# Fused RWKV-5 attention and SoLU feed-forward block on one core: early zeros, one product, the scalings and the last store move to other engines, and two small factors move behind a join

## Chip, cores and metric

One Trainium2 chip (trn2), one core. The metric is device time in microseconds (us), the median of several executions. Three runs of the kernel before gave 323.55, 321.37 and 322.94 us, so its median is 322.94 us.

## What is computed

The reference has two stages. The first is RWKV-5 attention over 4 batches, 8 heads, 768 positions and a head width of 48:

```python
for t in range(S):
    cur = einsum('bhd,bhe->bhde', u * k[t], v[t])
    y[t] = einsum('bhd,bhde->bhe', r[t], state + cur)
    state = w * state + einsum('bhd,bhe->bhde', k[t], v[t])
```

The second takes x, the 3072 rows of 384 that the heads of y form:

```python
h = x @ w_in                       # 384 -> 1024
solu = h * softmax(h)
ln = (solu - mean) / sqrt(var + 1e-6) * g_ln
out = ln @ w_out                   # 1024 -> 384
```

All of it is in 32-bit floats; w_in, w_out and g_ln come as 64-bit floats and are converted on the chip.

## The kernel before, in words

The rows are cut into N = 24 units of 128 positions (4 batches by 6 chunks of time). All of the work is in `direct_path`; the order of the instructions on each engine is the order in which the program text calls the helpers, written out by hand for all stages (no scheduler reorders it). An engine runs its queue in order, and waits at an instruction whose operands are not ready, so that everything behind it on that engine waits too.

A unit goes through these helpers. `load` (L471) issues the transfers of k, r and v on SP's queue. `decay_k` (L718) multiplies k by a table of decays, `kdec`, on GpSimd (POOL) and gives `kp` (L721); `decay_r` (L725) does the same for r. `weigh` (L732) forms the product r·k·u in two GpSimd multiplications, L734 (k by u) and L735 (times r), into `rku`; `sum_own` (L737) sums it over the head on VectorE (DVE, L739), and `diagonal` (L744) writes those sums onto the diagonal of the score tile, for the first four units by eight ScalarE (ACT) activations (L749). `turn_r` and `turn_k` (L774, L781) transpose r and kp on TensorE (PE); `whole_scores` (L794) or `scores` (L806) multiply them; `take_scores` (L822) copies the upper part of the scores over the diagonal tile on DVE (L827, L832). `whole_y` or `merged_y` multiply with v (L858, L881); `outer` builds the new state (L913) and `middle` and `update` add it (L934, L947, L949). `take_y` (L887) brings y to `xT` on ACT (L892); `ffn_in` (L962) multiplies it with w_in into the one `h_ps` tile (L969); `exponential` (L974) takes the exponential on ACT (L977), `unit_a` (L1046) forms solu on DVE (L1053), and only then can the next unit's `ffn_in` overwrite `h_ps`. `unit_b` (L1057) takes the squares on ACT (L1064, L1065). `halve_ln` (L1124) splits the words in halves (L1127), a transposing transfer turns them (L1116), and `join_ln` (L1130, L1121) puts the words together on DVE. `row_sums_12` (L1197) forms two sums of turned rows (L1201, L1202), which TensorE needs for the products in `both_a` to `both_d` (L1211) with w_out. `variance`, `root` and `shifts` (L1071, L1075, L1079) give the factors that `normalise` (L1098, ACT, L1102) applies.

Before the units stands the setup: an identity, tables of decays built by doubling on DVE (L648 to L654), `turn_table` (L662), which transposes a table on PE and copies it on ACT to `kdec` (L665), and the zeros: six tiles `vts` hold v, and their second halves (`vt[:, 1]`, 128 by 512 words) are zeroed by one ACT activation each (L641). ACT reaches the copy to `kdec` only behind the six. `spin` (L615) issues matmuls on PE whose result is not used.

The weights come in 14 pieces. `convert_a` to `convert_d` (L531 to L572) take the low words on ACT (L537), the high words on DVE (L550, L552), add on POOL (L560), and, for the eight pieces of w_out, scale by -g (`minus_g`): pieces of odd number on ACT (L568), of even number on DVE (L571). The scalings stand in the loop at L1399, in its four later passes, two pieces each.

At the end, `both_c` (L1265) and `both_d` (L1279) add up and store the last two units. For the last pair, `both_d` copies the left 192 columns on DVE (L1284) and stores them by SP (L1285). Every engine then reads a flag (L1842) and branches over a fallback path (L1843) that isn't taken; SP waits for all transfers and engines (L1870).

Of the kernel before, what the change touches and what calls it, by code (L numbers as in the profile page):

```python
# [9 lines left out]
F32 = mybir.dt.float32  # L10
# [389 lines left out]
def direct_path(  # L400
# [29 lines left out]
    nc = tc.nc  # L430
    B, H, S, D = r.shape
# [18 lines left out]
    apool = ctx.enter_context(tc.tile_pool(name="apool", bufs=2))  # L450
# [15 lines left out]
    NLD, NV = 5, 6  # L466
    rpads = [const.tile([128, H, P], F32, name=f"rpad{i}") for i in range(NLD)]
    kpads = [const.tile([128, H, P], F32, name=f"kpad{i}") for i in range(NLD)]
    vts = [const.tile([128, 2, H, P], F32, name=f"vt{i}") for i in range(NV)]
# [70 lines left out]
    def convert_b(j):  # L540
        hi, low = step[j]
        n = low.shape[1]
        ma = wpool.tile([128, n], U32, tag="ma", name="ma", bufs=4)
        part = ma
        if pieces[j][2] is None:
            part = psM.tile([128, n], F32, tag="m", name="part").bitcast(U32)

        nc.vector.tensor_scalar(out=part, in0=hi, scalar1=3, scalar2=0x3FFFFFF8,  # L550
                                op0=ALU.logical_shift_left, op1=ALU.bitwise_and)
        nc.vector.scalar_tensor_tensor(out=ma, in0=hi, scalar=0xC0000000, in1=part,  # L552
                                       op0=ALU.bitwise_and, op1=ALU.bitwise_or)
        step[j] = ma, low
# [8 lines left out]
    def convert_d(j, scalar=False):  # L563
        dst, _, f = pieces[j]
        ma, low = step.pop(j)
        if f is not None:
            if scalar:
                nc.scalar.activation(out=dst, in_=ma.bitcast(F32), func=ACT.Copy,  # L568
                                     scale=minus_g[:, f : f + 1])
            else:  # L570
                nc.vector.tensor_scalar_mul(out=dst, in0=ma.bitcast(F32),  # L571
                                            scalar1=minus_g[:, f : f + 1])  # L572
# [64 lines left out]
    u_ps = psM.tile([128, dm], F32, tag="m", name="u_ps")  # L637
    nc.tensor.matmul(u_ps, ones_row, u_row, start=True, stop=True)
    nc.scalar.copy(out=u_bc.rearrange("p h d -> p (h d)"), in_=u_ps)
    for vt in vts:  # L640
        nc.scalar.activation(out=vt[:, 1].rearrange("p h x -> p (h x)"),  # L641
                             in_=ident[:, 0:1].to_broadcast([128, H * P]), func=ACT.Copy, scale=0.0)
    nc.vector.tensor_scalar(out=pw[:, 0, 0], in0=wd_ps, scalar1=LOW, scalar2=HIGH,
# [2 lines left out]
    for j in range(8):  # L646
# [5 lines left out]
        else:  # L652
            n = 1 << (j - 1)
# [54 lines left out]

    ones = const.tile([128, 1], F32, name="ones")
    nc.gpsimd.memset(ones, 1.0)  # L710

    live = {}

# [4 lines left out]
    def decay_k(i):  # L718
        X = live.setdefault(i, {})
        X["kp"] = apool.tile([128, H, P], F32, name="kp", bufs=5)  # L720
        nc.gpsimd.tensor_mul(X["kp"].rearrange("p h d -> p (h d)"),  # L721
                             kpads[i % NLD].rearrange("p h d -> p (h d)"),
                             kdec.rearrange("p a d -> p (a d)"))
# [5 lines left out]
                             rpads[i % NLD].rearrange("p h d -> p (h d)"),  # L729
                             rdec.rearrange("p a d -> p (a d)"))  # L730

    def weigh(i, engine):  # L732
        rku = live[i]["rku"] = apool.tile([128, H, D], F32, name="rku")
        engine.tensor_mul(rku, kpads[i % NLD][:, :, 0:D], u_bc)  # L734
        engine.tensor_mul(rku, rku, rpads[i % NLD][:, :, 0:D])  # L735

    def sum_own(i):  # L737
        own = live[i]["own"] = small.tile([128, H, 1], F32, name="own")
# [223 lines left out]
    def ffn_in(i, halves=(0, 1), units=True):  # L962
        X = live[i]
        if 0 in halves:
            X["h"] = psH.tile([128, dff], F32, tag="h", name="h_ps")
        h_ps = X["h"]
        for n in halves:
            for j in range(KD):
                nc.tensor.matmul(h_ps[:, ts(n, NX)], X["xT"][:, j, :], w_in_sb[:, j, ts(n, NX)],  # L969
                                 start=(j == 0), stop=(j == KD - 1))  # L970
        if 1 in halves and units:
            exponential(i)
# [94 lines left out]
    def unit(i):  # L1067
        unit_a(i)
        unit_b(i)
# [9 lines left out]
    def shifts(i, j, engine):  # L1079
        i = max(i, SEVEN)  # L1080
        if i < j:
            tot, shift, scale, rstd = (stats[:, n, i:j] for n in (1, 2, 3, 4))
            engine.tensor_scalar(out=scale, in0=rstd, scalar1=-float(dff), scalar2=1.0,
                                 op0=ALU.mult, op1=ALU.mult)
            engine.tensor_tensor(out=shift, in0=tot, in1=rstd, op=ALU.mult)  # L1085
# [34 lines left out]
    def join(words, turned):  # L1120
        nc.vector.tensor_copy(out=words.bitcast(U16).rearrange("p n (t o) -> p o n t", o=2),  # L1121
                              in_=turned)
# [7 lines left out]
    def join_ln(i):  # L1130
        X = live[i]
        if i not in ROOM:
            X["lnT"] = fpool.tile([128, KF, 128], F32, name="lnT")
        else:
            X["lnT"] = bigs[ROOM[i]].rearrange("p (f t) -> p f t", f=KF)
        join(X["lnT"], X["turned"])
# [36 lines left out]
    KH, NH = KF // 2, dm // 2  # L1173
    left, right = slice(0, NH), slice(NH, dm)
# [34 lines left out]
    def block(dst, rows, weights, start=False):  # L1209
        for f in range(KH):  # L1210
            nc.tensor.matmul(dst, rows[:, f], weights[:, f], start=(start and f == 0),  # L1211
                             stop=(f == KH - 1), skip_group_check=True)
# [52 lines left out]
    def both_c(i):  # L1265
        X, Y = live.pop(i), live.pop(i + 1)
        ending[i] = X
        o, o2, a, e = (X[n] for n in ("o", "o2", "a", "e"))
        rows, rows2 = (out[ds(b * S + c * T, T)] for b, c in (units[i], units[i + 1]))
        if not X.get("summed"):  # L1270
            nc.vector.tensor_tensor(out=o2[:, right], in0=a, in1=o2[:, right], op=ALU.add)
        block(a, Y["lnT"][:, KH:KF], sums_w[4])
        if i + 2 == N:
            nc.sync.dma_start(out=rows2[:, right], in_=o2[:, right])
        if X.get("summed") != 2:
            nc.vector.tensor_tensor(out=o[:, right], in0=e, in1=o[:, right], op=ALU.add)
        nc.sync.dma_start(out=rows, in_=o)

    def both_d(i):  # L1279
        X = ending.pop(i)  # L1280
        (b, c), o2, a = units[i + 1], X["o2"], X["a"]
        rows2 = out[ds(b * S + c * T, T)]
        if i + 2 == N:
            nc.vector.tensor_copy(out=o2[:, left], in_=a)  # L1284
            nc.sync.dma_start(out=rows2[:, left], in_=o2[:, left])  # L1285
        else:
            nc.scalar.copy(out=o2[:, left], in_=a)
            nc.sync.dma_start(out=rows2, in_=o2)
# [31 lines left out]
    for q in range(2):  # L1320
        rows = slice(q * P, q * P + D)
        nc.gpsimd.tensor_tensor(out=wide.rearrange("p (a q) -> p a q", q=2)[P : P + D, :, q],
                                in0=back[rows, :, 0], in1=pw[rows, 0, 0], op=ALU.mult)
    weigh(0, nc.gpsimd)
    decay_k(0)
    sum_own(0)
    diagonal(0)
# [1 line left out]
    spin(2)  # L1329
    whole_scores(0)  # L1330
    convert_b(0)
    decay_k(1)
    weigh(1, nc.gpsimd)
    turn_r(1)
    spin(4)
# [63 lines left out]
    for i in range(LA, LA + LO):  # L1399
        j = i - LA  # L1400
        load(i + 5, "kr")
        load(i + 4, "v")
        if i > LA:
            ffn_in(j)
        before, now = now, [todo.pop(0) for _ in range(2 if todo else 0)]
        turn_r(i + 2)
        turn_k(i + 2)
        for p in before:
            convert_c(p)
        for p in now:  # L1410
            take_up(p)
        if i > LA:
            diagonal(i + 1)
            unit(j)
        for p in before:
            convert_d(p, p % 2)
        sum_own(i + 2)
        decay_k(i + 3)
        if i + 3 >= FIRST:
            decay_r(i + 3)  # L1420
        weigh(i + 3, nc.gpsimd)
        if i - LO >= 0:
            halve_ln(i - LO)
        if i - LO - 1 >= 0:
            join_ln(i - LO - 1)
        if i + 1 < WHOLE:
            whole_scores(i + 1)
            take_scores(i + 1)
        else:
            place(i + 1)  # L1430
            attend([i + 1])
            middle(i + 1)
        if LA < i < WHOLE:
            whole_y(i)
            take_y(i)
            whole_outer(i)
        elif i >= WHOLE:
            merged_y(i)
            take_y(i)
        if i > LA:  # L1440
            update(i)
        else:
            nc.vector.tensor_single_scalar(out=minus_g, in_=g_sb, scalar=-1.0, op=ALU.mult)
        if i + 1 >= WHOLE:
            take_scores(i + 1)
        for p in now:
            convert_b(p)
        halve_rk(i + 3)
# [17 lines left out]
    i = LA + LO  # L1466
    j, l = i - LA, 0
# [41 lines left out]
    for i in range(LA + LO + 2, ELEVEN, 2):  # L1509
        j, l = i - LA, i - LA - LO  # L1510
# [8 lines left out]
        first, second = ([n] if n < N else [] for n in (i + 2, i + 3))  # L1519
# [121 lines left out]
    for i in range(ELEVEN, N - 1, 2):  # L1641
        j, l = i - LA, i - LA - LO
        one, two = turned[i]
        first, second = ([n] if n < N else [] for n in (i + 2, i + 3))
# [80 lines left out]
    i = N - 1  # L1725
    j, l = i - LA, i - LA - LO
# [68 lines left out]
    variance(i, N, nc.vector)  # L1795
    root(i, N)
    both_c(l)
    shifts(i, N, nc.vector)
    join_ln(l + 3)
    row_sums_12(l + 2)  # L1800
    row_sums_34(l + 2, nc.vector)
    both_d(l)
# [72 lines left out]
```

## Time and profile before

The profile is of one execution of 322.73 us; its trace spans 321.0 us.

| What | us or share |
|---|---|
| median of three runs | 322.94 |
| the profiled execution, its own time | 322.73 |
| span of its trace | 321.0 |
| PE busy | 307.4 (96%) |
| DVE busy | 265.9 (83%) |
| POOL busy | 245.6 (77%) |
| ACT busy | 244.4 (76%) |
| transfers, mean share of the 16 engines, 22.3 to 56 us | 0.99 |
| granted TensorE clock | 0.996 |

How to read it. "Busy" is the time in which an engine has an instruction of that kind running. The slices of the page cut the span in 40; a table of stretches gives the same per stretch that one chooses. The chain of waits walks back from the last instruction to what released it. The timeline lists instructions with their start, duration, and the idle time before them with what ended it. Matmuls are counted twice in these rows (each 32-bit matmul leaves two records), and their ends are modelled.

### The profile page before, as it was taken

How to read it: one execution, taken by the hardware profiler on the slowest of the kernel's cores; microseconds unless marked ns; L12 is line 12 of the kernel's file. 1: busy time of each engine (PE TensorE's matmuls, PEld its weight loads, DVE VectorE, ACT ScalarE, POOL GpSimd, SP SyncE). 2: the span in 40 equal slices, each digit the busy share in tenths (PEclk: the TensorE clock that was granted, in tenths of full speed). 3: DMA queues.
4: the chain of work that ended last, by engine and by line, in shares of the span. 5: the costliest groups of instructions: out<-in, count | busy, mean ns of one | idle time of the engine just before them, and what ended most of it. 6: DMA issues, size and time to landing. Idle time of an engine off the chain costs nothing.

```text
span 321.0 us, 9696 instructions
## 1 busy us (share of the span) xinstructions
PE 307.4 (96%) x3903; PEld 216.9 (68%) x3903; DVE 265.9 (83%) x449; ACT 244.4 (76%) x418; POOL 245.6 (77%) x264
## 2 busy tenths in 40 slices
PE   6989999999999999999999999999999999999992
PEld 4866566555456466687677677678768677769891
DVE  7796999998887988989889799799979946777760
ACT  3875888888559888968968969959959968788420
POOL 3999778889999999999999999979988274272000
PEclk9999999999999999999999999999999999999998
DMA  7999998778999999988999999995876445675912
GB/s 161 241 266 208 200 188 205 119 142 134 190 170 178 173 175 150 162 145 169 165 196 180 168 191 209 197 196 114 143 174 144 85 121 118 135 191 116 204 76 61
DMA packets 165780, 52.64 MB, mean 164 GB/s; under 512 B 158301, under 2 KB 161502, under 8 KB 165726
## 3 DMA queue, kind: packets, MB, share of 16 engines
q1 hardware_dynamic: 165712, 51.92, 83.3%
q8 instruction: 33, 0.54, 0.7%
q14 instruction: 21, 0.17, 0.2%
q10 hardware_dynamic: 14, 0.00, 0.0%
HBM read 26.75 MB, written 4.72 MB: 98 GB/s over the span
## 4 chain that ended last, share of the span: by engine, by line
PE 61%; POOL 18%; DVE 10%; issue 4%; DMA 3%; SPq 1%; ACT 0%; POOLq 0%; ACTq 0%
PE o_ps L1211 26%; PE h_ps L969 16%; PE h_part L1003 9%; POOL kp L721 4%; POOL rku L734 4%; POOL big L754 3%; POOL rp L728 3%; PE y_ps L881 2%; POOL rku L735 2%; PE at L819 2%; DMA vt<-in_v_dram 1%; DVE ma L552 1%; PE h_part L881 1%; DMA wq<-in_w_dram 1%; DVE big L832 1%
## 5 line engine op out<-in xcount | busy, mean ns | idle before, releaser
L969 PE MATMUL h_ps<-w_in_sb,xT 128*128 128x512 f32 x216 | 96.9, 598 | 0.0
L969 PEld LDWEIGHTS h_ps<-w_in_sb,xT 128*128 128x128 f32 x216 | 39.9, 190 | 44.9 <-issue 43.2
L1127 ACT COPY halves<-solu 128x2048 uint16<-128x2048 uint16 x23 | 43.6, 1895 | 1.9 <-DMA halves<-halves 1.7
L721 POOL TENSOR_TENSOR kp<-kpad,kdec 128x512 f32<-128x512 f32 x24 | 34.1, 1423 | 0.9 <-ACT kdec L665 0.2
L1121 DVE COPY big<-halves 128x2048 uint16<-128x2048 uint16 x21 | 33.8, 1613 | 0.6 <-DMA halves<-halves 0.3
L1121 DVE COPY lnT<-halves 128x2048 uint16<-128x2048 uint16 x18 | 31.2, 1759 | 0.0
L735 POOL TENSOR_TENSOR rku<-rku,rpad 128x384 f32<-128x384 f32 x24 | 29.2, 1218 | 1.9
L832 DVE COPY_PREDICATED big<-later_half,at 64x512 f32<-64x512 uint32 x40 | 29.5, 736 | 0.7
L734 POOL TENSOR_TENSOR rku<-kpad,u_bc 128x384 f32<-128x384 f32 x24 | 29.8, 1241 | 0.2
L754 POOL TENSOR_SCALAR_AFFINE_SELECT big<-own 64x512 f32<-64x512 f32 x40 | 27.6, 691 | 1.8
L1211 PE MATMUL o_ps<-w_out_sb,ma 128*128 128x192 f32 x160 | 28.1, 328 | 0.0
L1211 PEld LDWEIGHTS o_ps<-w_out_sb,ma 128*128 128x128 f32 x160 | 26.2, 190 | 1.9 <-issue 1.6
L728 POOL TENSOR_TENSOR rp<-rpad,rdec 128x512 f32<-128x512 f32 x15 | 25.1, 1674 | 0.0
L977 ACT ACTIVATE e<-h_ps 128x1024 f32<-128x1024 f32 x18 | 18.4, 1022 | 8.7 <-PE h_ps L969 8.6
L1061 ACT ACTIVATE e<-solu,stats 128x1024 f32<-128x1024 f32 x20 | 23.0, 1148 | 2.2 <-DVE solu L1053 2.1
L1053 DVE SCALAR_TENSOR_TENSOR solu<-h_ps,stats,e 128x1024 f32<-128x1024 f32 x18 | 23.1, 1284 | 1.5
L1102 ACT ACTIVATE solu<-solu,stats 128x1024 f32<-128x1024 f32 x17 | 21.0, 1233 | 1.0 <-POOL stats L1085 0.9
L1166 PE MATMUL o_ps<-w_out_sb,lnT 128*128 128x384 f32 x64 | 21.6, 491 | 0.0
L1072 POOL TENSOR_SCALAR stats<-stats 128x2 f32<-128x2 f32 (+2 forms) x13 | 5.9, 451 | 19.2 <-ACT e L1061 18.7
L956 POOL TENSOR_TENSOR vt<-vt,wide 48x384 f32<-48x384 f32 x16 | 19.4, 1226 | 0.8
L1211 PE MATMUL o_ps<-w_out_sb,lnT 128*128 128x192 f32 x112 | 19.8, 330 | 0.0
L1211 PEld LDWEIGHTS o_ps<-w_out_sb,lnT 128*128 128x128 f32 x112 | 18.2, 190 | 1.7 <-issue 1.4
(198 smaller groups left out, 699.2 us busy)
## 6 DMA issues: line engine op xcount, KB each, us to landing
raw<-in_moe_w_out_dram SPq DMA_DIRECT2D x16, 384.0 KB, 4.1
kpad<-in_k_dram SPq DMA_DIRECT2D x24, 192.0 KB, 5.1
rpad<-in_r_dram SPq DMA_DIRECT2D x24, 192.0 KB, 5.0
vt<-in_v_dram SPq DMA_DIRECT2D x40, 96.0 KB, 3.6
raw<-in_moe_w_in_dram SPq DMA_DIRECT2D x7, 512.0 KB, 6.7
out_dram<-o SPq DMA_DIRECT2D x18, 192.0 KB, 3.0
raw<-in_moe_w_in_dram SPq DMA_DIRECT2D x10, 256.0 KB, 3.8
out_dram<-kp SPq DMA_DIRECT2D x5, 192.0 KB, 2.5
```

The lines of the kernel that those rows point to most:

```text
L721: nc.gpsimd.tensor_mul(X["kp"].rearrange("p h d -> p (h d)"), kpads[i % NLD].rearrange("p h d -> p (h d)"), kdec.rearrange("p a d -> p (a ...
L728: nc.gpsimd.tensor_mul(X["rp"].rearrange("p h d -> p (h d)"), rpads[i % NLD].rearrange("p h d -> p (h d)"), rdec.rearrange("p a d -> p (a ...
L734: engine.tensor_mul(rku, kpads[i % NLD][:, :, 0:D], u_bc)
L735: engine.tensor_mul(rku, rku, rpads[i % NLD][:, :, 0:D])
L754: nc.gpsimd.affine_select(out=G[rows, c].rearrange("p a q u -> p (a q) u"), in_=X["own"][rows].to_broadcast([U, H, U]), compare_op=ALU.is_ ...
L832: nc.vector.copy_predicated(X["G"][rows, c].rearrange("p a q u -> p q a u"), later_half[rows].unsqueeze(1).to_broadcast([U, 2, HP, U]), X[ ...
L969: nc.tensor.matmul(h_ps[:, ts(n, NX)], X["xT"][:, j, :], w_in_sb[:, j, ts(n, NX)], start=(j == 0), stop=(j == KD - 1))
L1003: nc.tensor.matmul(dst, rows, weights, start=start, stop=True, skip_group_check=True)
L1053: nc.vector.scalar_tensor_tensor(out=solu, in0=X["h"], scalar=rs, in1=X["e"], op0=ALU.mult, op1=ALU.mult, accum_out=tot)
L1121: nc.vector.tensor_copy(out=words.bitcast(U16).rearrange("p n (t o) -> p o n t", o=2), in_=turned)
L1127: copy(out=both.rearrange("p (o n) -> p o n", o=2), in_=split(X["solu"]))
L1211: nc.tensor.matmul(dst, rows[:, f], weights[:, f], start=(start and f == 0), stop=(f == KH - 1), skip_group_check=True)
```

## The change

Six edits. (1) Only the first four v tiles get their zeros on ACT; the two others get them from two GpSimd memsets, placed behind the last of its setup memsets. (2) `weigh` takes a second engine; for unit 0 the multiplication by r is done by DVE. (3) `decay_k(1)` moves from behind `convert_b(0)` to directly behind `weigh(0)`, ahead of `decay_k(0)`. (4) All scalings of the w_out pieces go to ACT. (5) Behind `both_c` of units 18 and 19, `join_ln(l + 3)`, the join of unit 21, comes before `shifts(i, N, nc.vector)`, the factors of the last unit (L1798, L1799). (6) The last store of 192 columns is cut in two halves of 96: the first is copied by DVE and stored by SP, the second is copied by ACT and stored by ACT's queue.

```diff
-    for vt in vts:
+    for vt in vts[:4]:
         nc.scalar.activation(out=vt[:, 1].rearrange("p h x -> p (h x)"),
...
     nc.gpsimd.memset(ones, 1.0)
+    for vt in vts[4:]:
+        nc.gpsimd.memset(vt[:, 1], 0.0)
...
-    def weigh(i, engine):
-        rku = live[i]["rku"] = apool.tile([128, H, D], F32, name="rku")
+    def weigh(i, engine, second=None):
+        rku = live.setdefault(i, {})["rku"] = apool.tile([128, H, D], F32, name="rku")
         engine.tensor_mul(rku, kpads[i % NLD][:, :, 0:D], u_bc)
-        engine.tensor_mul(rku, rku, rpads[i % NLD][:, :, 0:D])
+        (second or engine).tensor_mul(rku, rku, rpads[i % NLD][:, :, 0:D])
...
         if i + 2 == N:
-            nc.vector.tensor_copy(out=o2[:, left], in_=a)
-            nc.sync.dma_start(out=rows2[:, left], in_=o2[:, left])
+            for n, (copy, store) in enumerate(((nc.vector.tensor_copy, nc.sync),
+                                               (nc.scalar.copy, nc.scalar))):
+                part = slice(n * NH // 2, (n + 1) * NH // 2)
+                copy(out=o2[:, part], in_=a[:, part])
+                store.dma_start(out=rows2[:, part], in_=o2[:, part])
...
-    weigh(0, nc.gpsimd)
+    weigh(0, nc.gpsimd, nc.vector)
+    decay_k(1)
     decay_k(0)
     sum_own(0)
...
     convert_b(0)
-    decay_k(1)
     weigh(1, nc.gpsimd)
...
         for p in before:
-            convert_d(p, p % 2)
+            convert_d(p, True)
         sum_own(i + 2)
...
     both_c(l)
+    join_ln(l + 3)
     shifts(i, N, nc.vector)
-    join_ln(l + 3)
     row_sums_12(l + 2)
```

## The prediction

> **What bounds the kernel now.** The busy shares of the page come first: PE is busy for 96% of the span, so only the stretches where PE stands still can give time back. The table of stretches shows where they are (columns: length, then PE, PEld, DVE, ACT, POOL busy with instruction counts, clock, transfer share, GB/s):
>
> ```profile
> 0.00:22.30 22.30, 17.85 (x255) 14.73 (x255) 17.46 (x58) 14.11 (x33) 16.41 (x34) 1.00 0.94 229
> 22.30:56.00 33.70, 33.70 (x475) 20.46 (x472) 29.91 (x57) 27.04 (x59) 27.79 (x29) 1.00 0.99 197
> 56.00:75.00 19.00, 17.39 (x323) 10.31 (x325) 18.35 (x32) 16.77 (x28) 16.29 (x17) 1.00 0.71 127
> ...
> 291.00:299.00 8.00, 7.44 (x46) 7.17 (x45) 7.01 (x15) 6.90 (x8) 0.68 (x2) 1.00 0.44 101
> ```
>
> PE lacks 4.45 us up to 22.3, nothing up to 56, 1.6 us from 56 to 75, 0.56 us from 291 to 299, and the last 6 us; the rows left out here (75 to 291) lack 0.8 in all. Second, PE's waits over the span (us in total, times, longest), which name who ends those gaps:
>
> ```profile
> PE kv_ps L913 <- DVE big L779: 1.3, 2, 0.7
> PE y_ps L858 <- issue: 0.7, 1, 0.7
> PE o_ps L1211 <- DVE ma L1202: 0.6, 1, 0.6
> ```
>
> The two on L779 lie at 58.1 and 67.3, with one of 0.3 on L832 at 74.6; the one on L1202 lies at 298.5.
>
> Third, the chain of waits for the start (start, us, what), and ACT's timeline beside it:
>
> ```profile
> 8.46 1.01 POOL rku L734
> 9.54 1.00 POOL rku L735
> 10.54 0.17 issue
> 10.74 2.52 POOL kp L721 x2
> ```
>
> ```profile
> 6.97 3.22 ACT L641 ACTIVATE vt<-ident 128x512 f32<-128x512 f32 x6
> 10.09 0.57 ACT L665 COPY kdec<-kd_ps 128x512 f32<-128x512 f32 x1
> ```
>
> From 8.5 to 15.3 us the chain is GpSimd's; kp needs kdec, which ACT copies only behind six zeroings. The chain is also GpSimd's from 67 to 121 us, where the change adds and removes nothing of GpSimd's; PE then runs from 128.4 to 291.
>
> **What the Trainium skill says.** "ScalarE: Activation LUTs" (What ACT_TABLE_LOAD costs) prices an activation at 186 ns + 0.833 ns per element, 93 ns more for a pointer scale: 599 ns for 384 columns; the trace's L568 takes 600. "SBUF — State Buffer" (SBUF: two separate sides) calls the pair of ports that DVE and GpSimd share an exclusive lock, held for a whole instruction, also by a DVE instruction with two SBUF inputs against GpSimd reads; that bears on the product moved to DVE. The trace agrees in kind: L728 takes 1.29 us at 77.2 and 2.33 us beside DVE's copy L1121 at 70 us. "DMA: Bandwidth & Descriptors" (Issuing engines are not separate DMA queues) says that a second queue saves only the issue time; no transfer of the trace before shows two queues near the end.
>
> **The change part by part.**
>
> Zeros, the product and the order at the start. Two zeroings less on ACT are 2 x 0.54 = 1.07 us (3.22/6): ACT is free at 9.1 instead of 10.1. kdec can then start once its transposes end: PE's kd_ps runs 8.25 to 9.31, so kdec runs about 9.36 to 9.93. GpSimd's two memsets: small ones show 98 ns for one column and 194 for 128, so 512 columns are about 0.48 us each, 1.0 in all; GpSimd idles 4.0 us before 7.94, waiting for the tables, and hides them. On DVE the product has no row of this shape; L1201, the same kind with 512 columns, takes 0.69, and smaller rows drop about 1 ns a column, so 0.55 us. Bounds: 0.5, or 1.5 if it waits for a GpSimd instruction of 1 us. DVE idles 1.39 us before L739, so it runs 9.55 to 10.1, and sum_own starts at 10.1 instead of 10.57; ACT's eight activations start 0.45 us earlier. Nothing else stands behind the product's wait on DVE before the product itself is ready (L790 ends at 9.19). kp starts at about 10.1 (the lock until the product ends) instead of 10.74: 0.6 us, though 1.0 us left GpSimd, because kdec gates. The later rows on GpSimd and DVE shift by 0.6. The new order of decay_k puts unit 1's kp 1.3 us earlier still, ready at 11.4, where PE asks for it at 13.1; kp(0) is then ready at 12.6, and its reader on PE comes at 15.5. No transfer gates: the weight piece that lands last, issued at 13.45, needs 9.1 us and is there at 22.55, DVE takes it at 24.32. PE itself idles in this stretch, behind something that moves, 0.16 (tk_ps at 13.31), 0.34 and 0.16 us (y_ps at 19.46 and 20.04): 0.66. Its 0.73 before 21.63 ended by nothing the profile names, and I leave it there. So PE can gain 0 to 0.9; I take 0.5, carried to 56, since PE has no gap there.
>
> Scalings. Four DVE instructions of 0.55 (L571, 2.2 us) become four on ACT of 0.60 less the 0.09 overlap of neighbours (2.0 to 2.4 us). ACT in passes 3 to 6, by its timeline: the exponential L977 waited 1.0 and 0.7 us for PE after the first two, which hides 0.6 us each. In the third it did not wait:
>
> ```profile
> 61.71 0.60 ACT L568 ACTIVATE w_out_sb<-ma,minus_g 128x384 f32<-128x384 f32 x1
> 62.22 1.88 ACT L1127 COPY halves<-solu 128x2048 uint16<-128x2048 uint16 x1
> ...
> 66.05 1.01 ACT L977 ACTIVATE e<-h_ps 128x1024 f32<-128x1024 f32 x1
> ```
>
> PE had finished h_ps at 65.04, so ACT was 1.0 us late, and each 0.6 more goes through L977 to DVE's L1053 (67.51), then to PE's next h_ps (68.86). Against this, DVE is 0.55 earlier at L1053 of that pass (58.14), which released ACT's L1064 (ACT idle 0.88 there). So ACT comes to L977 about where it did. The gap at 58.1 closes (0.66 less 0.1), but the next (67.27, DVE behind the v transfer that lands at 61.2) stays, and h_ps then waits for L1053 as before: most of the gain is given back. At 74.57 DVE's 0.46 of the fourth L571 closes PE's 0.3. In the fourth pass L977 at 75.46 goes to 76.0, and DVE's L1053 with it; PE has other work there (L1166 until 80.8), which hides it. Bounds: 0.6 lost to 1.6 gained; I take 0.2 gained.
>
> Factors behind the join. DVE's rows:
>
> ```profile
> 294.70 0.35 DVE L1276 TENSOR_TENSOR kp<-o_ps,kp 128x192 f32<-128x192 f32 x1
> 295.45 0.15 DVE L1083 TENSOR_SCALAR stats<-stats 128x1 f32<-128x1 f32 x1 [0.40 <-POOL stats L1076]
> ```
>
> DVE stands 0.40 us for GpSimd's root, then comes L1085 (0.15), and the join L1121 at 295.58 (1.32). Behind the join instead, the join (its transfer landed at 292.1) runs from 295.07 to 296.37, the two factors to 296.6, and L1201 starts there instead of 296.94: 0.33 us at PE's gap of 0.56. The price: ACT's L1102 needs the factors and would have started at 296.48, now 296.67. That is 0.2 us later for the last unit's split and its transposing transfer, which landed at 304.45, just when DVE took it (304.47); row sums are then ready at 307.5 where PE, 0.33 earlier, asks at 307.4. So 0.25 (bounds 0 and 0.4).
>
> Last store. The rows before:
>
> ```profile
> 314.85 0.36 DVE L1284 COPY kp<-o_ps 128x192 f32<-128x192 f32 x1 [0.94 <-PE o_ps L1211]
> 315.24 0.69 SPq L1285 DMA_DIRECT2D out_dram<-kp  x1
> ```
>
> ```profile
> L1843 ACTq EVENT_SEMAPHORE  x1: 17/17/17, 315.7 to 315.7; - x1
> L1843 SPq COMPARE_BRANCH  x1: 58/58/58, 316.3 to 316.3; - x1
> ```
>
> Half the columns cost DVE 0.26 (0.36 less 0.1), so SP issues at 315.14. In the built order ACT's copy waits for DVE, not PE: it runs 315.15 to 315.4 (0.32 for 192 columns, less 0.08), ACT issues then (SP's issues take 0.33 to 0.69), reads the flag (0.48) and branches. A branch takes about 2.9 us on ACT (312.8 to 315.7), so ACT is through at 319.4 to 319.8; SP's own branch, 316.3 to 319.0, sets the end, and it asks for ACT only after 319.7. Landing (2.7 us) ends before. So 0.1 gained; bounds 0.45 (SP's issue shrinks to 0.33) and a loss of 0.5 (ACT's first issue took 1.27).
>
> Sum: 322.73 - 0.5 - 0.2 - 0.25 - 0.1 = 321.7 for an execution like the profiled one. The median is 0.2 above it, so 321.9.
>
> **Rivals.** (a) The start's gain does not reach PE. For: transfers are at 0.94 to 0.99 of the 16 engines until 56, and the unnamed 0.73. Against: the landings I find up to 25 us have over a microsecond to spare. 322.4. (b) DVE's relief passes on, both waits on L779 and the one on L832 go (1.6 us), and 1.2 us of it lasts. For: DVE is busy 18.35 of 19.0 us there. Against: ACT's late L977. 322.94 - 0.85 - 1.2 = 320.9. (c) Slower: ACT becomes late. Place: L977 at 66 and 75 us. Price: the two added scalings there, 0.6 each, and, since ACT's other work of the passes shifts, nothing given back: 1.2 lost, and the 0.2 not gained. 321.9 + 0.2 + 1.2 = 323.3. It decides once more than 0.85 us of them (the other parts' gains: 0.5, 0.25 and 0.1) reach h_ps. (d) The halves cost the end 0.5: 322.5; goes with (a).
>
> **How the numbers follow.** The main case has 0.46 (321.9, its own range 321.2 to 322.6, as single executions differ by up to 2.2 us), (a) with (d) 0.18, (b) 0.24, (c) 0.12. The range 320.4 to 323.2 leaves out half of (c) and the tail of (b). A measurement of this kernel tells about 1% (3.2 us) from no change: all gaps together, 0.66 + 1.6 + 0.56 + 0.45, are 3.3 us, so faster by over 1% has 0.05; slower 0.02; the same 0.93.
>
> **What would show it.** Right: kdec before 9.5, y_ps of unit 1 near 19.5, L977 of the third pass near 65.5 with its 1.0 us of lateness kept, PE's gap at 298.2 near 0.25, the SP issue 0.35 us behind PE's last matmul. Wrong: no gap left from 56 to 75, a new wait of h_ps on L1053, or ACT's semaphore after SP's at the end.

## The result and the profile after

The changed kernel takes 321.42 us (median of 22 runs, 319.87 to 324.99), the kernel before 322.48 beside it (22 runs, 321.37 to 323.76): a ratio of 0.9963, 95% interval 0.9946 to 0.998. (The ratio leaves out the run of 324.99 us, a slow one, more than 1.5% above the fastest.) That is 1.06 us between the medians, where 1.05 had been predicted; the parts of that sum are another matter, and the experiments are about them. Line numbers after are 2 higher than before from L713 on (L721, L734, L779 and L788 are L723, L736, L781 and L790) and 6 higher behind the last store.

The table of stretches of the kernel after, the same columns and stretches as shown of before:

```profile
0.00:22.30 22.30, 18.96 (x287) 15.78 (x287) 18.43 (x60) 14.36 (x33) 16.80 (x36) 1.00 1.03 233
22.30:56.00 33.70, 33.66 (x450) 19.93 (x449) 29.84 (x55) 28.02 (x59) 28.45 (x28) 1.00 1.03 203
56.00:75.00 19.00, 17.81 (x354) 10.63 (x354) 16.69 (x30) 17.16 (x30) 16.82 (x17) 1.00 0.62 112
...
291.00:299.00 8.00, 7.77 (x48) 7.47 (x48) 7.50 (x15) 6.97 (x9) 1.47 (x1) 1.00 0.46 109
```

PE lacks 3.34 us up to 22.3 (4.45 before), 1.19 from 56 to 75 (1.61), 0.23 from 291 to 299 (0.56). Between 75 and 128.4 it lacks 0.07 where before it lacked 0.32. PE's waits over the span (us in total, times, longest) show what ends the gaps now:

```profile
PE y_ps L883 <- issue: 0.7, 1, 0.7
PE y_ps L883 <- ACT big L790: 0.7, 1, 0.7
PE y_ps L860 <- issue: 0.4, 2, 0.2
PE kv_ps L915 <- DVE big L781: 0.3, 1, 0.3
PE o_ps L1213 <- ACT kp L1230: 0.2, 1, 0.2
```

One of the two waits on L781 (then L779) is down from 0.66 to 0.28, the other has become a wait of y_ps on ACT, 0.69 us at 67.2, and the wait on DVE's row sum L1204 (then L1202) at 298 is a wait of 0.2 on ACT. At the start, the timelines of ACT (first two rows) and DVE:

```profile
9.10 0.58 ACT L665 COPY kdec<-kd_ps 128x512 f32<-128x512 f32 x1 [0.19 <-PE kd_ps L664]
10.54 0.69 ACT L751 ACTIVATE big<-ident,own 128x128 f32<-128x128 f32 x2 [0.85 <-DVE own L741]
```

```profile
9.36 0.56 DVE L737 TENSOR_TENSOR rku<-rku,rpad 128x384 f32<-128x384 f32 x1 [0.32 <-POOL rku L736]
9.95 0.55 DVE L741 TENSOR_REDUCE own<-rku 128x8 f32<-128x384 f32 x1
```

kdec is copied at 9.10 instead of 10.09, of which 0.25 us is not the change's: the transposes that it needs began 0.25 earlier in this execution. The product takes 0.56 us on DVE. At the end, SP issues its half after DVE's, ACT its own after both:

```profile
L1291 SPq DMA_DIRECT2D out_dram<-kp x1: 427/427/427, 313.7 to 313.7; - x1
...
L1291 ACTq DMA_DIRECT2D out_dram<-kp x1: 393/393/393, 314.0 to 314.0; - x1
```

```profile
L1849 SPq EVENT_SEMAPHORE  x8: 17/17/17, 317.2 to 317.7; - x8
...
L1849 SPq COMPARE_BRANCH  x1: 58/58/58, 314.5 to 314.5; - x1
...
L1849 ACTq EVENT_SEMAPHORE  x1: 17/17/17, 318.0 to 318.0; - x1
```

From PE's last matmul (its end, 313.39) to the end of the span, 319.1, are 5.7 us; before they were 6.2.

### The profile page after: what moved, and what is told of

The parts are those of the page before. It is cut to its first block, busy times and chain, and to the rows that moved or that the text cites. A ratio compares the mean times of both kernels' runs of the same rounds, so it can differ in the third digit from the quotient of the medians.

```text
span 319.1 us, 9700 instructions
## 1 busy us (share of the span) xinstructions
PE 307.8 (96%) x3903; PEld 217.0 (68%) x3903; DVE 263.1 (82%) x446; ACT 246.2 (77%) x421; POOL 246.8 (77%) x265
## 4 chain that ended last, share of the span: by engine, by line
PE 74%; POOL 8%; DVE 6%; ACT 4%; issue 3%; DMA 2%; SPq 1%; ACTq 0%; POOLq 0%
PE o_ps L1213 26%; PE h_ps L971 21%; PE h_part L1005 9%; PE y_ps L883 3%; PE at L821 2%; POOL rku L736 2%; POOL rp L730 2%; PE o_ps L1168 2%; PE at L803 2%; POOL kp L723 1%; PE y_ps L860 1%; DVE solu L1055 1%; PE h_part L883 1%; PE tr_ps L780 1%; DMA rpad<-in_r_dram 1%
## 5 line engine op out<-in xcount | busy, mean ns | idle before, releaser
L723 POOL TENSOR_TENSOR kp<-kpad,kdec 128x512 f32<-128x512 f32 x24 | 34.1, 1422 | 1.1 <-ACT kdec L665 0.4
L834 DVE COPY_PREDICATED big<-later_half,at 64x512 f32<-64x512 uint32 x40 | 29.5, 738 | 0.7
L737 POOL TENSOR_TENSOR rku<-rku,rpad 128x384 f32<-128x384 f32 x23 | 28.5, 1240 | 1.8
L736 POOL TENSOR_TENSOR rku<-kpad,u_bc 128x384 f32<-128x384 f32 x24 | 29.8, 1240 | 0.2
L979 ACT ACTIVATE e<-h_ps 128x1024 f32<-128x1024 f32 x18 | 18.4, 1020 | 7.9 <-PE h_ps L971 7.7
```

Source lines behind the costliest of these rows:

```text
L737: (second or engine).tensor_mul(rku, rku, rpads[i % NLD][:, :, 0:D])
L834: nc.vector.copy_predicated(X["G"][rows, c].rearrange("p a q u -> p q a u"), later_half[rows].unsqueeze(1).to_broadcast([U, 2, HP, U]), X[ ...
```

## Experiments: each part alone

Each of the first four kernels is the kernel before with one part of the change, made by that part's lines of the diff. The first has the zeros, the product and the order of the start:

```
-    for vt in vts:
+    for vt in vts[:4]:
...
+    for vt in vts[4:]:
+        nc.gpsimd.memset(vt[:, 1], 0.0)
...
+    weigh(0, nc.gpsimd, nc.vector)
+    decay_k(1)
```

> Only edits 1 to 3 (zeros of two tiles on GpSimd, the product of unit 0 on DVE, unit 1's kp first). My theory: kdec starts near 9.1 to 9.4 instead of 10.1, unit 1's y near 19.5 instead of 20.0, and PE carries 0.5 to 1.0 us to its first h_ps (23.3 before) and on to the end, since PE has no gap from there to 56: 0.5 to 1.0 us faster than before. Rival (a), the start's gain lost on the way: under 0.2 us faster, with h_ps of later passes back at the old times (33.5, 42.1, 50.5 us).

Measured: 322.78 us against 322.72, a ratio of 1.0002 (0.998 to 1.0025). No gain. Its trace shows one way in which the gain arrives and is lost. h_ps begins at 23.02 instead of 23.33 and is 0.3 ahead until 41.76; between there and the next h_ps it loses 0.9. First DVE's timeline, then GpSimd's, then PE's, all of this kernel:

```profile
41.27 1.43 DVE L571 TENSOR_SCALAR w_out_sb<-ma,minus_g 128x384 f32<-128x384 f32 x1
42.62 0.54 DVE L741 TENSOR_REDUCE own<-rku 128x8 f32<-128x384 f32 x1
```

```profile
41.20 1.28 POOL L723 TENSOR_TENSOR kp<-kpad,kdec 128x512 f32<-128x512 f32 x1
42.44 1.12 POOL L736 TENSOR_TENSOR rku<-kpad,u_bc 128x384 f32<-128x384 f32 x1
```

```profile
49.50 0.57 PE L915 MATMUL kv_ps<-vt,kp 64*48 64x48 f32 x30 [0.76 <-DVE big L781]
```

DVE's scaling takes 1.43 us, because it comes 0.07 us behind the start of GpSimd's kp. In the kernel before the same two stood the other way round, scaling first (DVE's timeline of before, then GpSimd's):

```profile
41.59 0.53 DVE L571 TENSOR_SCALAR w_out_sb<-ma,minus_g 128x384 f32<-128x384 f32 x1
```

```profile
41.99 1.27 POOL L721 TENSOR_TENSOR kp<-kpad,kdec 128x512 f32<-128x512 f32 x1
```

GpSimd is 0.79 us ahead of the profile before there and DVE only 0.32, and so the scaling comes behind kp. "SBUF — State Buffer" of the Trainium skill (SBUF: two separate sides) has it that the pair of ports that the two engines share is an exclusive lock, held for the whole instruction of the one that starts first. The traces agree: of the 26 scalings that DVE runs in these kernels, 24 end 0.21 or 0.22 us behind the end of the GpSimd instruction that was running when they began, the other two 0.31. So the 0.53 us of before is itself in large part a wait, for a GpSimd instruction that ended at 41.91, and the 1.43 is a longer one, for kp until 42.48. DVE is then 0.9 later, and PE has a wait of 0.76 that no other kernel here has.

That is one profile, of an execution of 323.34 us, 0.56 above this kernel's median, so it doesn't show that every execution loses its gain so. Nor is it shown that the start's edits put DVE behind kp: among the eight kernels of the table further down, DVE comes to this place behind the start of kp in three, the three whose gap of PE at 21 us is longest (1.20, 1.21 and 1.48 us), and one of these has none of the start's edits. Over many executions it stays open what takes the gain away.

The second kernel has the scalings alone, `convert_d(p, True)`:

> Only edit 4 (all scalings of w_out on ACT). My theory: PE's gap on L779 at 58.1 closes (0.5 us), most of it is given back at 67 to 69 us, where PE then waits for ACT; 0.2 us faster (0.6 slower to 0.6 faster). Rival (b), the relief of DVE passes on: both gaps on L779 go and 1.0 us or more is kept. Rival (c): PE waits longer than before between 65 and 69 us and the kernel is 0.5 us or more slower.

Measured: 322.39, ratio 0.9987 (0.9971 to 1.0003). PE lacks 1.36 us from 56 to 75 instead of 1.61, and 0.12 instead of 0.32 up to 128.4: 0.45 us less. The wait of 0.69 us on ACT's L788 is there too.

The third has the join before the factors, the two lines swapped:

> Only edit 5 (the join ahead of the last unit's factors). My theory: PE's gap of 0.56 before the products at 298.5 shrinks to 0.2 or 0.25, so the products start 0.3 us earlier relative to PE's block before; the last turned rows become the next thing DVE waits for, 0.1 to 0.5 us, without PE waiting for them. 0.25 us faster. Rival: the later turned rows stop PE near 307 and the gain is 0.

Measured: 322.61, ratio 0.9989 (0.9973 to 1.0005). The time by itself says little; the gap is clear. PE's timeline of this kernel:

```profile
298.47 1.57 PE L1211 MATMUL o_ps<-lows,ma 128*128 128x192 f32 x8 [0.23 <-ACT kp L1228]
```

It was 0.56 and ended by DVE's L1202; 0.23 is left, and what ends it is ACT.

The fourth has the store in two halves:

> Only edit 6 (the last store in two halves). My theory: from PE's last matmul to the end of the span it takes 5.7 us instead of 6.2, because SP issues 0.1 us earlier, its issue takes 0.4 instead of 0.7, and SP's branch sets the end; 0.1 to 0.5 us faster. Rival (d): ACT, which now issues and branches last, ends behind SP, and the end is the same or up to 0.5 us later.

Measured: 322.34, ratio 0.9988 (0.997 to 1.0006). The end needs more than one profile. SP's issue of the last store begins 0.42 or 0.43 us behind PE's last matmul in six kernels that store it whole and 0.32 in eight with halves: the shorter copy gives its 0.1 every time. The issue itself then takes 0.42 to 1.26 us in the six and 0.43 to 0.86 in the eight, so half the columns do not make it reliably shorter. From PE's last matmul to the end of the span the six have 5.74 to 6.90 us, mean 6.12, the eight 5.72 to 6.68, mean 6.06.

## Experiments: what the parts do to each other

The changed kernel without the three edits of the start:

> The changed kernel without the three edits at the start: scalings, join and store alone. The start alone gave a ratio of 1.0002. Theory A (the start's gain is eaten whatever else is changed, by the PE gap before the last y_ps of unit 1 that ends with no named releaser): the same as the changed kernel, a ratio of 0.996 to 0.997. Theory B (alone, the start loses its gain because it puts VectorE's scaling at 41.3 us beside GpSimd's kp, 1.43 us instead of 0.53; the scalings moved to ACT take that away): the start is worth something beside the scalings, this kernel is 0.4 to 0.9 us slower than the changed one, a ratio of 0.9975 to 0.999.

Measured: 322.05 against 322.73, ratio 0.997 (0.9954 to 0.9986). The changed kernel has 0.9963, so the start is worth 0.2 us beside the other parts, give or take 0.8 (both intervals added as squares). Neither theory is ruled out by this pair.

The changed kernel with the even pieces of the last two passes back on DVE:

```
-            convert_d(p, True)
+            convert_d(p, i < LA + 3 or p % 2)
```

> The changed kernel, but in the last two of its four passes the even pieces are scaled on VectorE again. Theory (ACT's extra scalings are what the new wait of 0.69 us at 67.2 us is made of): ACT comes to L790 0.55 us earlier there, VectorE's L781 0.33 us later (0.55 less the 0.22 that it idles), so the wait of y_ps on ACT shrinks to about 0 and the one of kv_ps to about 0.5, and the kernel is 0.3 to 0.4 us faster than the changed one: 321.0 to 321.1 where the changed one gives 321.4 beside a before of 322.5, a ratio near 0.995. Rival (VectorE is the bound of these passes, as in the kernel before): both waits on L781 come back with 0.66 us and the ratio is 0.998. Second rival: the gain ends in PE's idle time behind GpSimd near 128 us, and the time is the changed kernel's.

Measured: 321.70, ratio 0.9965 (0.9947 to 0.9982): the changed kernel's time, as the second rival had it, and not 0.3 to 0.4 us less. On PE the first rival's mechanism is there for one of its two waits on L781; the other stayed at 0.28. PE's waits of this kernel:

```profile
PE y_ps L860 <- issue: 1.2, 1, 1.2
...
PE kv_ps L915 <- DVE big L781: 0.9, 2, 0.7
PE y_ps L883 <- issue: 0.8, 1, 0.8
...
PE o_ps L1213 <- DVE stats L1051: 0.3, 1, 0.3
PE at L821 <- DVE big L834: 0.3, 1, 0.3
```

The 0.69 and 0.17 on ACT are gone; 0.66 on L781, 0.31 on L834 and 0.32 on L1051 are back. My estimate had DVE 0.33 late at L781 and it is 0.66 late, as in the kernel before. With four pieces on ACT the waits from 56 to 128 sum to 0.28 + 0.17 + 0.69 = 1.14, with two to 0.28 + 0.66 + 0.31 + 0.32 = 1.57, with none to 0.66 + 0.66 + 0.30 + 0.32 = 1.94. So the fourfold move is the best of the three on PE, by 0.4 us that the times of these two do not resolve.

## Experiments: the gap that nothing named

PE's gap before unit 1's last y_ps, put down to "issue", was left out of the prediction. It lies before the last four of the same 32 matmul records in eight profiles (a matmul leaves two records, each with a weight load). The queue q8 carries transfers of kind "instruction", 16 KB each; the span after has 32 of them, for PE's 7806 recorded matmuls and weight loads, one for every 250 or so. From the traces, in us:

| kernel | PE ready | q8's transfer ends | PE goes on |
|---|---|---|---|
| before | 20.90 | 20.26 | 21.63 |
| scalings alone | 20.93 | 20.24 | 21.54 |
| join alone | 20.67 | 20.23 | 21.67 |
| store alone | 20.93 | 20.61 | 21.97 |
| all but the start | 20.73 | 21.01 | 22.21 |
| start alone | 20.11 | 19.91 | 21.31 |
| even pieces half back | 20.30 | 19.99 | 21.51 |
| after | 20.40 | 19.28 | 20.63 |

PE goes on 1.20 to 1.52 us behind the end of that transfer, whenever it was ready. The Trainium skill's "Runtime: NRT & Kernel Launch" (Instruction fetch mechanics) says that each engine fetches its own instructions in blocks of 16 KiB, 256 instructions, and that the cost of crossing into a block is mostly hidden. The block size agrees; here PE stands up to 1.48 us, while the 16 transfer engines are full (a mean busy share of 0.94 to 1.03 up to 22.3 us in these traces). Near 213 us the same kind of gap (0.18 to 0.78 us in the eight) follows another such transfer by 1.33 to 1.58 us. A count settles more: between the two gaps lie 5376 recorded instructions of PE (matmuls, weight loads and those of its sequencer) in each of the eight traces, which is 21 times 256, and q8 ends exactly 21 transfers from the one to the other.

If this is a wait for instructions, more records ahead of it must move it. Six kernels with more records were made; the matmuls they add write a tile that nothing reads. First, twelve of one column, 24 matmul records, in the changed kernel and in the kernel before:

```
+        for _ in range(thin):
+            nc.tensor.matmul(ps[:, 0:1], ident, ident[:, 0:1], start=True, stop=True)
...
+    spin(3, 12)
```

> The changed kernel with 12 one-column matmuls more behind the three at the very start, where PE idles 1.2 us for a transfer; nothing else depends on them. The gap of PE before the last four of unit 1's 32 y_ps matmuls lies at the same instruction in six profiles, and PE goes on 1.30 to 1.44 us behind the end of a 16 KB transfer of the queue of kind instruction. Theory (PE waits for its own next block of instructions): 24 records more (two each) move the gap 24 matmuls forward, to behind the first four of unit 1's y_ps, where VectorE's copy is waited for anyway; the block is asked for some 2 us earlier, so the gap of 0.2 to 1.2 us goes or shrinks to under 0.3, and the kernel is 0.3 to 1.0 us faster than the changed one: a ratio of 0.993 to 0.9955. Rival (the gap belongs to the data of these four matmuls, by a wait that the profile doesn't name): it stays before the last four y_ps, and the time is the changed kernel's, 0.996 to 0.997.

Measured: 324.44, ratio 1.0042 (1.0024 to 1.006).

> The kernel before with the same 12 one-column matmuls more. If PE's gap at 21.6 us (0.73) is its next block of instructions, it moves to behind the first four y_ps of unit 1, and h_ps begins 0.5 to 0.7 us earlier (22.6 to 22.8 instead of 23.3); since passes 58 and 67 still wait for VectorE, part is given back: 0 to 0.6 us faster, a ratio of 0.998 to 1.0. Rival (the gap is data): gap and time as before, ratio 1.000.

Measured: 325.60, ratio 1.008 (1.005 to 1.011). Both slower, for a reason of their own. PE's timeline of the first:

```profile
2.85 5.12 PE L621 MATMUL spin<-ident 128*128 128x1 f32 x24
7.90 0.27 PE L638 MATMUL wd_ps<-ident,wq 4*128 4x4 f32 x1
```

A record takes 213 ns here though it has but one column, and PE comes to h_ps at 25.27, 2.9 us later than in the profile after. Of the waits put down to "issue", 0.16 at most is left in front of y_ps and none near 213. The first proves nothing, since PE came to it late; the second speaks for the theory, since a PE that is late also asks later, and yet the transfer of the same number (the 22nd) ended at 205.09 and 203.88 us instead of 211.40 to 212.76.

The same with twelve of 64 columns, with and without the start's edits; the estimate of 35 ns a record was wrong too:

> The changed kernel with 12 matmuls of 64 columns more (side by side in the tile that the first three write, read by nothing) in PE's idle 1.2 us at the start. The twelve of one column took 213 ns a record, 5.1 us for 24, and made PE 2.9 us late at the start, so they could not tell the fetch's gap from PE's lateness; records of 64 columns take about 35 ns in this trace, so these should take 0.9 to 1.3 us and fit. Theory (PE waits for its next block of instructions): the block is asked for 24 records, some 1.5 us, earlier; the gap before the last four y_ps of unit 1 (1.2 us in two profiles with this start, 0.23 in the profiled execution of the change) is gone, none above 0.3 takes its place, h_ps begins at 21.9 to 22.4; the gap near 213 us goes from its instruction too. Time: 0.5 to 1.0 us faster than the changed kernel, a ratio of 0.993 to 0.995. Rival (data): gap and time as in the changed kernel, 0.9963.

Measured: 323.71, ratio 1.0015 (0.9993 to 1.0037).

> The same 12 matmuls of 64 columns in the changed kernel without its edits of the start (zeros, product, order). Theory (the start's gain of about 0.5 us is real on PE and was eaten only by the wait for instructions): with that wait gone, PE comes to h_ps 0.5 us later than with the start's edits, at 22.4 to 22.9, and this kernel is 0.3 to 0.7 us slower than the one with them; it is itself faster than the same without the 12 matmuls (0.997), a ratio of 0.9945 to 0.9965. Rival (the start's edits are worth nothing even so, because VectorE and GpSimd set the pace until 130 us): the two shifted kernels agree within 0.2 us.

Measured: 324.68, ratio 1.0046 (1.0027 to 1.0064). The 24 records took 5.22 us in both. Against each other the two are a measurement of the start's edits without a wait for instructions: h_ps begins at 25.38 and 25.85, and the times differ by 0.97 us (give or take 0.9).

Last, idle matmuls that exist already, 4 and 3 of 128 rows, replaced by 12 and 9 of 32 rows, in the changed kernel and in the kernel before:

```
-    spin(4)
+    spin(12, 32)
...
-    spin(3)
+    spin(9, 32)
```

> The changed kernel in which two of the groups of idle matmuls, 4 and 3 of 128 output rows at 12 and 14 us, become 12 and 9 of 32 rows. In this trace a record with 128 rows of weights takes 0.11 us and one with 32 rows 0.036 us, so both groups keep their length (0.9 and 0.7 us), but PE has 28 records more behind it before unit 1's y_ps, without the 3.2 us that the earlier kernels with more records paid before 10 us, where every record took 0.21 us whatever its width. Theory (wait for instructions): the gap of 1.2 us before the last four y_ps goes (under 0.3 at the start of y_ps), h_ps begins at 21.8 to 22.4, the gap near 213 us (0.5 to 0.8) goes too as in the four kernels with 24 records more; the kernel is 0.7 to 1.5 us faster than the changed one, a ratio of 0.992 to 0.9945. Rival (GpSimd's and VectorE's pace until 130 us gives nothing back): h_ps begins earlier, PE waits more at 57 to 67 us or at 128, and the time gains only the gap near 213: a ratio of 0.9945 to 0.996. Second rival (the gap is data): 0.9963 as the changed kernel.

Measured: 323.10, ratio 1.0004 (0.9981 to 1.0026).

> The same replacement of idle matmuls in the kernel before. Theory: the gap of 0.73 at 21.6 us and the one of 0.47 at 213.9 us go, h_ps begins at 22.5 to 22.9 instead of 23.3; 0.5 to 1.2 us faster than before, a ratio of 0.9965 to 0.9985. Together with the same replacement in the changed kernel it says what the change is worth when no wait for instructions eats the start's gain: the theory expects the whole change at 1.3 to 1.8 us there (1.06 without), the rival at about 1.0.

Measured: 324.54, ratio 1.0052 (1.0037 to 1.0067). PE's timeline of the first of the two:

```profile
12.15 2.81 PE L619 MATMUL spin<-ident 128*32 128x128 f32 x24
14.89 0.66 PE L788 MATMUL tk_ps<-ident,kp 128*128 128x128 f32 x4
15.47 2.04 PE L619 MATMUL spin<-ident 128*32 128x128 f32 x17
```

24 records take 2.74 us until the next line starts, 114 ns each; the 36 ns that I took from y_ps hold for y_ps, which has the same shape but writes side by side where these write one place again and again (why it differs was not tried). So these too made PE late, at 24.85 and 24.40 instead of 22.3 to 23.9, and the gain that was looked for was never offered. The gap near 213 is gone in all six kernels, with the 22nd transfer at 201.74 to 205.09 us. So the gaps lie a whole number of blocks apart, they end at a fixed distance behind a transfer, and the one that could be tested went when the count of instructions ahead of it changed: that they are waits for instructions is well supported. A version in which PE has more records and no lateness was not found, so what the two gaps cost the kernel's time stays open. Between these two the whole change is worth 1.44 us, give or take 0.9.

## Why the prediction came out right, point by point

**Start, 0.5 of the sum: right on PE, wrong in what carries it.** PE is ready for the last y_ps of unit 1 at 20.83 in the mean of the five profiles without the start's edits and 20.27 in the three with them: 0.56 us. kdec at 9.10 (9.36 predicted, its transposes were 0.25 earlier in this execution), the product 0.56 (0.55), kp at 9.76 (10.1, behind the product; it began while the product ran until 9.92 and took 1.29 us, against 1.28 before, so this lock cost next to nothing). Two things failed. The gap "ended by nothing the profile names", which was left there, is a wait whose end PE's own earliness does not set alone; the profiled execution after had it at 0.23 with its transfer 0.6 to 1.7 us earlier than the others', and so shows a whole microsecond gained where 0.65 is the mean (h_ps: 23.50 without the start, 22.86 with). And "carried to 56, since PE has no gap there" looked at PE alone: in the profile of the start alone GpSimd moved 0.79 and DVE 0.32, and they collided at 41.3. Rival (a), the gain that does not reach the end, is what the start does by itself (1.0002). In that profile PE was ready 0.79 us earlier than before; the unnamed gap, which (a) had among its reasons, took 0.47 of it (1.20 instead of 0.73), and the collision, which the prediction did not name, 0.9. In the whole change this collision cannot happen, because the scaling has left DVE; there the start is worth 0.2 us by one pair and 1.0 by the other, give or take 0.8 and 0.9, which is no more than a hint that the 0.5 was about right. That the scalings are what saves it is argued, and weakly: in the trace after, DVE comes to this place at 40.90, ahead of kp at 41.26, so a scaling there would not have met it. Start and scalings together, without the rest, were not run.

**Scalings, 0.2: too small on PE, and by the wrong gap.** The gap at 58 closed to 0.28, not 0.1. The step that failed is "ACT comes to L977 about where it did". These are PE's and ACT's rows after:

```profile
58.52 5.42 PE L971 MATMUL h_ps<-w_in_sb,xT 128*128 128x512 f32 x12
```

```profile
60.60 1.11 ACT L568 ACTIVATE w_out_sb<-ma,minus_g 128x384 f32<-128x384 f32 x2
...
65.44 1.01 ACT L979 ACTIVATE e<-h_ps 128x1024 f32<-128x1024 f32 x1
66.47 0.20 ACT L979 ACTIVATION_READ_ACCUMULATOR e<-h_ps 128x1 f32 x1
66.58 0.57 ACT L790 COPY big<-tk_ps 128x512 f32<-128x512 f32 x1
```

PE ends h_ps at 63.94 and L979 (then L977) starts 1.5 us later, where it was 1.0 before and was to stay so: the second scaling adds 0.51 to ACT. DVE did come 0.35 us earlier to L1053 of that pass in the trace of the scalings alone (57.79 instead of 58.14), but PE's h_ps came 0.35 earlier too, so ACT won nothing against PE. With the scaling back on DVE the lateness is 1.0 again (64.50 and 65.50). "The next (67.27) stays", on DVE, and h_ps waiting for L1053 were wrong as well: DVE's wait went there and ACT took its place, not through L977 and h_ps but through L790 behind it, 0.69 against 0.66. Rival (c)'s mechanism, ACT late, therefore exists with nearly its size, and rival (b)'s too: on PE they cancel at 67 and leave the gaps at 58 and 74.6, and 0.32 before 128.4 that the prediction counted only among "0.8 in all". Together 0.45 us in the trace of the scalings alone and 0.67 in the trace after, within the bounds of 0.6 lost and 1.6 gained.

**Join, 0.25: right.** The gap went from 0.56 to 0.23 alone and in the whole, 0.33 us. GpSimd's root took 1.47 us instead of 0.55 at 293.8 and lay hidden behind the join. The price is as it was said too: in the trace of the join alone DVE waits 0.40 us for the last turned rows, and PE doesn't.

**Store, 0.1: right in size as far as it shows.** SP's issue begins 0.1 us earlier in all eight profiles with halves, 0.32 behind PE's last matmul (0.35 predicted); what follows it varies by more, and the means to the end differ by about 0.05 us over fourteen profiles. One sign that was to show it wrong is there, ACT's semaphore at 318.0 behind SP's 317.7; but SP's closing instructions run on from 317.79 to 319.07, 1.28 us, as before (1.29, 319.66 to 320.95), so it cost nothing in this execution.

That the sum was met to 0.01 us is luck. The scalings brought more than was said, and the start, beside them, perhaps what was said; on PE the parts come to some 1.6 us (0.56, 0.67, 0.33 and 0.05), and the two profiled executions differ by 1.87. The 1.06 between the medians has an interval of 0.6 to 1.7, so no part of it is confirmed by the sum alone, and where the rest of PE's gain goes in other executions stays open.

## What to carry to other kernels

Before an edit brings one of two engines that share ports ahead, look at the whole stretch behind it for pairs that change their order: in one profile, with GpSimd 0.8 us and VectorE 0.3 us ahead, an instruction of VectorE of 0.53 us took 1.43, 30 us behind the edit. A wait that the profile puts down to "issue", always before the same instruction, is to be held against the instruction queue's transfers, and the instructions between two such waits are to be counted, before it is left out of a sum. Where two engines are both nearly full, moving work between them trades one wait for another, and the sum of PE's waits over the whole stretch, not the one gap, is what to price.

## What the runs showed that was not expected

Up to about 10 us a matmul record of this kernel took 0.21 us, with 1, 64 or 128 columns, and 0.114 us at 12 to 15 us with 32 rows or 128; 32-row records of y_ps, written side by side, follow at 0.036 us. At the two gaps put down to its instructions PE went on 1.2 to 1.6 us behind the end of a 16 KB transfer, and the gaps lie 21 times 256 recorded instructions apart. A scaling on VectorE of 0.42 to 1.43 us ended 0.21 to 0.31 us behind a GpSimd instruction, whatever its own length. SP's issue of one and the same 96 KB store took between 0.42 and 1.26 us.
